# A second batch's queries turned by DMA instead of on TensorE, in a fused attention and feed-forward kernel

## The chip, the core and the metric

The kernel runs on one core of a Trainium2 chip. A core has TensorE (PE, with its weight loads shown apart as PEld), VectorE (DVE), ScalarE (ACT), GpSimd (POOL) and SyncE (SP), each with an instruction queue of its own, and 16 DMA engines that move data between memories. Matmuls read SBUF and write PSUM. The metric is the device time of one execution in microseconds (us); lower is better. The profile is of one execution: its span runs from the first to the last instruction.

## What is computed

Linear attention without a softmax on q, k, v of shape (batch 8, heads 8, sequence 576, head width 64), a normalization per head, and then a feed-forward network on the 4608 tokens with 512 features:

```
kv  = einsum('bhsd,bhse->bhde', k, v)            # 64 x 64 per batch and head
o   = einsum('bhsd,bhde->bhse', q, kv)
x   = o / sqrt(mean(o*o, -1) + 1e-6) * g_norm    # heads side by side: 4608 x 512
a, b = x @ w1, x @ w2                            # 4608 x 1024 each
out = (a * b) @ w3 @ w_out                       # 4608 x 512
```

The weights come as 64-bit floats and are converted to fp32 on the chip, in integer steps. w3 and w_out are multiplied once into one matrix (w3o).

## The kernel before

A batch has 576 tokens: 512 form a group of their own, and the 64 left of each batch are joined, two batches at a time, to a ninth group. The groups run in the order 0 to 6, 8, 7. Ahead of group 0 a start-up stage converts weights, folds w3 and w_out, and does batch 0's attention.

**A group's stages.** `gates(T, p, ...)` (blocks p = 0 to 3) computes a quarter of the hidden features by a scheme of seven products in place of eight (`winograd`), whose matmuls are L620 in the profile. Inside a block the products follow one another as: first product, copied by ScalarE as p1; second, copied as p5; third, added on top of the first in PSUM, copied as u2; fourth; fifth, copied as u3; sixth; seventh. The copies are `keep` (L633) and are remembered in `copies["u2"]` and so on. A PSUM bank that was copied is added to by a later product, so that the third product waits for p1's copy, the fourth for p5's, the fifth for u2's and the seventh for u3's. u2 and u3 share one SBUF buffer: u3's copy waits until VectorE has used u2. VectorE adds the parts (c, L758) and multiplies a and b (L755, L759). After the four blocks of group 0 comes its projection (`project`), later groups have `project_twice`.

**The next batch's attention inside a group.** `winograd` calls `between()` twice, and each call runs the next of eight places of `steps(T + 1)`. `steps` fills lists: `fs[i]` holds what is begun at place i, and `ends[i]` what is ended there, ahead of it. In group 0 the first block runs no places, so that the second block holds places 0 and 1, the third 2 and 3, the fourth 4 and 5, and the projection 6 and 7. For batch 1 the places hold: kv = k^T v of a pair of head pairs (`begin_kv`, L334, copied out of PSUM at L345); the queries turned, so that the head width lies along partitions (`begin_q` with `q_t`, L353, copied at L355; `q_t_left`, L370 and L371, for the 64 left of batches 0 and 1 together); the product of queries and kv with the normalization (`finish`, `product`, L417; `product_left`, L436); the result turned for the gates (`turn`, L451, or `x_by_dma`).

**The other way to turn.** From batch 2 on the queries are turned by DMA with `turn_by_dma` (L275). A generator in three steps: GpSimd copies the low and the high 16-bit halves of the fp32 words apart into two planes (L292, L294); SP issues a DMA transpose of 16-bit elements (L296); GpSimd copies the halves together again (L306). `q_two_by_dma` drives two of these and loads the next queries (`load_ahead`) in the third step.

**Weights.** `begin_next()` does ScalarE's part of a conversion (L159, L160), `end_next()` VectorE's part (L162 to L172), in group 0 with a scaling on ScalarE (L135), and loads the next raw weights. Four conversions are left for group 0: two after block 0, two after block 1 (L1312 to L1318). `sum_w(3)`, which needs the last two, is run after block 2 and serves block 3.

**Order.** TensorE, GpSimd and SP run in the order of the program. VectorE and ScalarE are ordered by a planner at compile time, which takes what it expects to be ready and prefers what the program lists first; `tc.issue_after(ins)` puts the instructions of the block behind `ins` on the engine of `ins`. From group 1 on, VectorE too follows the order of the program in each group's last block and projection. For odd batches (b = 1, 3, 5) `steps` hands VectorE's copy to the next batch's `begin_kv`, so that the kv of batches 2, 4 and 6, heads 0 to 3, are copied by VectorE; others are copied by ScalarE.

Of the kernel before, what the change touches and what calls it, by code (L numbers as in the profile page):

```python
# [4 lines left out]

# [8 lines left out]
FP32 = mybir.dt.float32  # L14
# [9 lines left out]
def kernel(  # L24
# [32 lines left out]
    nc = tc.nc  # L57
    PSUM = bass.MemoryType.PSUM
    P = 128
# [4 lines left out]
    NP = H // 2  # L64
# [19 lines left out]
    def bank(pool, tag):  # L84
        return pool.tile([P, 512], FP32, name=tag, tag=tag)


    loaded, copies = {}, {}
# [161 lines left out]
    def all_of(steps):  # L250
        for _ in steps:
            pass
# [19 lines left out]
        for _ in range(n):  # L272
            nc.tensor.matmul(t[:, 0:P], lhsT=ident, rhs=ident, start=True, stop=True)

    def turn_by_dma(srcs, apart, turned, dsts):  # L275

        def words(t):  # L280
            return t.bitcast(U16).rearrange("p ... (n w) -> p ... n w", w=2)

        def planes(t, i, n):
            t = t.bitcast(U16).rearrange("p (w n) -> p w n", w=2)
            size = 4 * P // n
            return t[:, :, i * size:(i + 1) * size]

        for i, src in enumerate(srcs):
            to = planes(apart, i, len(srcs))
            if len(src.shape) == 3:  # L290
                src, to = words(src), to.rearrange("p w (a n) -> p w a n", a=src.shape[1])
                nc.gpsimd.tensor_copy(to, src.rearrange("p a n w -> p w a n"))  # L292
            else:
                nc.gpsimd.tensor_copy(to, words(src).rearrange("p n w -> p w n"))  # L294
        yield
        nc.sync.dma_start_transpose(  # L296
            out=turned.bitcast(U16).rearrange("p (a t) -> p a t", t=P), in_=apart.bitcast(U16)
        )
        yield
        for i, dst in enumerate(dsts):  # L300
            src = planes(turned, i, len(dsts))
            if len(dst.shape) == 3:
                src = src.rearrange("p w (a n) -> p a n w", a=dst.shape[1])
            else:
                src = src.rearrange("p w n -> p n w")
            nc.gpsimd.tensor_copy(words(dst), src)  # L306

    def together(turns):

# [6 lines left out]
    def attention(b):  # L316
        kv_b = kv_sb[b % 3]
        qT = {}

        def start():  # L320
            xT[b] = work.tile([P, 2, 2, NP // 2, N], FP32, name="xT")

        def kv(rs, copy=nc.scalar.copy):


            n = len(rs)
            kv_ps = bank(ps_at, "at")[:, 0:n * D].rearrange("p (r d) -> p r d", d=D)
            for r in rs:
                k_sb, v_sb = loaded["k", b, r], loaded["v", b, r]
                kl, vl = kv_left  # L330
                for j in range(J + 1):
                    cols = slice(j * D, (j + 1) * D)
                    for e in range(2):
                        nc.tensor.matmul(  # L334
                            kv_ps[e * D:(e + 1) * D, r - rs[0], :],
                            lhsT=k_sb[:, e, cols] if j < J else kl[:, 2 * r + e, :],
                            rhs=v_sb[:, e, cols] if j < J else vl[:, 2 * r + e, :],
                            start=(j == 0),
                            stop=(j == J),
                        )  # L340
            for e in range(2):
                for i in range(2):
                    dst = kv_b[i * D:(i + 1) * D, e, rs[0]:rs[0] + n, :]
                    src = kv_ps[e * D:(e + 1) * D]
                    copy(dst, src)  # L345

        def q_t(r):

# [8 lines left out]
        def q_by_dma(r):  # L357

            qT[r] = work.tile([P, 2, 2, P], FP32, name="qT")
            q_sb = loaded["q", b, r].rearrange("p e n -> p (e n)")  # L360
            to = qT[r].rearrange("p e i t -> p (e i t)")
            return turn_by_dma([q_sb], to, q_sb, [to])

        st = {}

        def q_t_left():
            st["qT"] = work.tile([P, NP, P], FP32, name="qT_left", bufs=1)
            qt_ps = bank(ps_at, "at").rearrange("p (r t) -> p r t", r=NP)
            for r in range(NP):
                nc.tensor.transpose(qt_ps[:, r, :], q_left[b // 2][:, 2 * r:2 * r + 2, :], ident)  # L370
            nc.scalar.copy(st["qT"], qt_ps)  # L371

        def q_left_by_dma():
            st["qT"] = work.tile([P, NP, P], FP32, name="qT_left", bufs=1)
            src = q_left[b // 2].rearrange("p h d -> p (h d)")
            to = st["qT"].rearrange("p r t -> p (r t)")
            return turn_by_dma([src], to, src, [to])

        def norm(o_ps, dsts):

# [102 lines left out]
                if r + 1 == NP and "k" in names:  # L483
                    load_kv_left(b + 1)

        def begin_kv(*rs, **how):
            kv(rs, **how)
            for r in rs:
                load_ahead("kv", r)

# [14 lines left out]
        def finish(h):  # L505
            all_of(product(h))

        return SimpleNamespace(**{f.__name__: f for f in (
            start, begin_kv, begin_q, product, finish, turn, q_t_left, product_left,
            q_two_by_dma, q_left_by_dma, x_by_dma, x_left_by_dma,  # L510
        )})

# [2 lines left out]
    def batch(b):  # L515
        if b not in batches:
            batches[b] = attention(b)
        return batches[b]

    def steps(b):  # L520

        a = batch(b)
        a.start()
        more = b + 1 < B
        fs, ends = ([[] for _ in range(8)] for _ in range(2))

        def turn(i, f, *args, next_group=False):  # L530

            t = []

            def begin():
                t.append(f(*args))
                next(t[0])
                next(t[0])

            fs[i].append((begin,))
            (to_end if next_group else ends[i + 1]).append((lambda: all_of(t[0]),))  # L540

        if to_end:

            ends[0] += [(lambda: nc.gpsimd.tensor_copy(tick, late["p5"][:, 0, 0:1]),), *to_end]
        to_end.clear()
        odd = b % 2
        if b == 1:
            fs[0] += [(a.begin_kv, 0, 1), (a.begin_q, 0, 1)]
        fs[1] += [(a.begin_kv, 2, 3), (a.finish, 0)]
        if b == 1:  # L550
            fs[2] += [(a.q_t_left,), (a.begin_q, 2, 3)]
            fs[3] += [(a.turn, 0), (a.turn, 1)]
        else:
            turn(1, a.q_two_by_dma, 2, 3)
            turn(2, a.x_by_dma, 0)
            if odd:
                turn(1, a.q_left_by_dma)
        second = 5 if b == 1 else 4
        if more:
            how = dict(copy=nc.vector.tensor_copy) if odd else {}  # L560
            fs[second].append((partial(batch(b + 1).begin_kv, **how), 0, 1))
        fs[second].append((a.finish, 1))
        if odd:
            fs[second].append((a.product_left,))
        if b == 1:
            turn(6, a.x_by_dma, 1)
            turn(7, a.x_left_by_dma, next_group=True)
        else:
            turn(5, a.x_by_dma, 1)
            if odd:  # L570
                turn(5, a.x_left_by_dma, next_group=more)
        if more:
            turn(7 if b == 1 else 5, batch(b + 1).q_two_by_dma, 0, 1, next_group=True)
            fs[7 if odd else 0].append((load_q_left, b + 1))
        return iter([lambda s=e + f: [f(*args) for f, *args in s] for e, f in zip(ends, fs)])

    to_end = []


    w3T = {}  # L580
# [683 lines left out]
    for n, T in enumerate(groups):  # L1264
        pieces = steps(T + 1) if n + 2 < NG else iter([])

        def between():
            next(pieces, lambda: None)()
            if T == 1:
                for _ in range(2):  # L1270
                    if next(preparing, 0) == 0 and len(loaded_b) < 3:
                        load_b()
            if T == B - 2 and p == 2 and not replaced:
                replaced.append(True)
                replace_a21()
# [11 lines left out]
        for p in range(NF):  # L1287
            if T in TWICE and p + 1 < NF:
                continue
            if T and p + 1 == NF:  # L1290
# [16 lines left out]
                gates(T, p, between, lambda name: all_of(f() for f in following[name]))  # L1307
                continue
            gates(T, p, between if T or p else lambda: None)
            if T == 0:  # L1310
                if p + 1 < NF:
                    run(sum_w(p + 1))  # L1312
                for n in range(2):
                    if len(converted) < len(todo):
                        ahead = [copies["xT"] if p == 0 else copies["u3"][0], copies["u2"][p]][n]
                        with tc.issue_after(ahead.ins):
                            begin_next()
                        end_next()  # L1318
                if p + 1 == NF:
                    allocate_projection()  # L1320
                    run(*(f(i) for i in range(NF) for f in (sum_ab, combine_w3o)))
            else:
                ops = [step() for step in sum_ab(p)]
                with tc.issue_after(ops[-1].ins):
                    for _ in range({(3, 1): 2, (3, 2): 2, (4, 1): 2, (4, 2): 1}.get((T, p), 0)):
                        next(preparing_w)
# [43 lines left out]
```

## Time and profile before

| | |
|---|---|
| three timed runs, us | 762.75, 763.65, 763.81 (median 763.65) |
| span of the profiled execution, us | 762.3 |
| group 0's gates and projection | about 85 to 168 us |
| TensorE's granted clock | full throughout |
| L353, transposes of queries | 32 in all (16 in the start-up stage), 278 ns mean |
| L355, L371: copies of these from PSUM, ScalarE | 8 at 594 ns, 1 at 597 ns |
| L345, kv copies | 52 on ScalarE, 260 ns mean |
| DMA transposes (L296) | 57, SP's queue |

In the profile's lines, L12 is line 12 of the kernel; a group reads: line, engine, operation, output<-inputs, shapes, count, and busy time or mean. A timeline's line begins with start and length in us, and its bracket tells how long the engine was idle before and what ended that. "PE at" is TensorE writing a bank of the pool `at` (attention), "PE mm" one of the pool `mm`. Busy durations of TensorE's instructions overlap, so that eight transposes of 0.27 us each can pass in less than 1 us of the chain.

### The profile page before, as it was taken

The page shows a single profiled execution, that of the slowest core. Times are in us where ns is not written, and L with a number is a line of the kernel's source. Part 1 is how long each engine was busy: PE and PEld are TensorE (multiplying, and loading weights), DVE is VectorE, ACT ScalarE, POOL GpSimd, SP SyncE. Part 2 cuts the span into 40 slices and gives each one's busy share as a digit, 9 for nine tenths or more (in the row PEclk, how much of TensorE's full clock was granted, in tenths as well). Part 3 has the DMA queues.
Part 4 walks back from the last instruction along what each step waited for, and adds up shares of the span by engine and source line. Part 5 has one row for each costly group of instructions (what it writes and reads, how often), then busy time and mean ns, then how long its engine had stood idle before and what let it go on. Part 6 is the DMA issues. An engine that isn't in the chain of part 4 may idle for free.

```text
span 762.3 us, 15002 instructions
## 1 busy us (share of the span) xinstructions
PE 753.6 (99%) x5943; PEld 661.1 (87%) x5943; DVE 593.9 (78%) x1183; ACT 251.7 (33%) x471; POOL 165.2 (22%) x190
## 2 busy tenths in 40 slices
PE   7999999999999999999999999999999999999998
PEld 5455788888899889988998899889988999999997
DVE  7977999548879468948984998467867777996897
ACT  6776764213321322233222222332233223222321
POOL 0000000123520442043204420432053115006100
PEclk9999999999999999999999999999999999999999
DMA  9996642328998935685668467835652471456244
GB/s 312 342 329 207 205 124 57 84 70 262 319 275 293 240 98 155 238 210 152 192 229 219 147 185 232 209 104 157 229 135 54 139 223 49 145 201 194 85 148 142
DMA packets 137049, 140.83 MB, mean 185 GB/s; under 512 B 77076, under 2 KB 124308, under 8 KB 136980
## 3 DMA queue, kind: packets, MB, share of 16 engines
q1 hardware_dynamic: 134528, 125.46, 55.5%
q10 hardware_dynamic: 2452, 14.42, 5.5%
q8 instruction: 47, 0.77, 0.4%
q14 instruction: 22, 0.18, 0.1%
HBM read 105.78 MB, written 19.14 MB: 164 GB/s over the span
## 4 chain that ended last, share of the span: by engine, by line
PE 96%; DMA 2%; DVE 1%; ACT 0%; issue 0%; SPq 0%; ACTq 0%
PE mm L620 54%; PE mm L1049 22%; PE mm L599 7%; PE mm L849 5%; PE at L334 3%; PE at L417 2%; DMA raw<-in_moe_w_out_dram 1%; PE at L849 1%; DMA w3o_sb<-w3o_l 1%; PE at L586 1%; PE at L353 1%; PE at L1100 0%; DVE kv_sb L345 0%; DMA raw<-in_moe_w_dram 0%; PE at L451 0%; PE at L436 0%
## 5 line engine op out<-in xcount | busy, mean ns | idle before, releaser
L620 PE MATMUL mm<-xT,w_sb 128*128 128x256 f32 x720 | 165.2, 379 | 0.0
L620 PEld LDWEIGHTS mm<-xT,w_sb 128*128 128x128 f32 x720 | 136.3, 190 | 18.7 <-issue 0.5
L620 PE MATMUL mm<-xc,ws 128*128 128x256 f32 x512 | 115.7, 379 | 0.0
L620 PEld LDWEIGHTS mm<-xc,ws 128*128 128x128 f32 x512 | 97.2, 190 | 13.3
L758 DVE TENSOR_TENSOR c<-mm,u 128x512 f32<-128x512 f32 x32 | 22.0, 688 | 63.2 <-PE mm L620 63.2
L292 POOL COPY xT<-xn 128x1024 uint16<-128x1024 uint16 x26 | 31.6, 1244 | 177.9 <-DVE xn L395 177.9
L633 ACT COPY u<-mm 128x512 f32<-128x512 f32 x58 | 34.1, 587 | 99.2 <-PE mm L620 90.6
L633 ACT COPY p<-mm 128x512 f32<-128x512 f32 x66 | 38.7, 586 | 77.9 <-PE mm L620 75.0
L599 PE MATMUL mm<-chunks,ab 128*128 128x512 f32 x128 | 60.3, 603 | 2.0 <-ACT ab L591 1.3
L620 PE MATMUL mm<-xc,w_sb 128*128 128x256 f32 x256 | 61.4, 383 | 0.0
L620 PE MATMUL mm<-xT,ws 128*128 128x256 f32 x240 | 57.3, 382 | 0.0
L759 DVE TENSOR_TENSOR ab<-c 128x256 f32<-128x256 f32 x96 | 54.3, 566 | 2.5
L620 PEld LDWEIGHTS mm<-xc,w_sb 128*128 128x128 f32 x256 | 47.8, 190 | 6.9 <-ACT u L633 0.3
L620 PEld LDWEIGHTS mm<-xT,ws 128*128 128x128 f32 x240 | 44.9, 190 | 6.2
L1049 PE MATMUL mm<-w3o_sb,ab 128*128 128x128 f32 x368 | 48.7, 275 | 0.0
L1049 PE MATMUL mm<-w3o_sb,raw 128*128 128x128 f32 x372 | 48.1, 275 | 0.3 <-DMA w3o_sb<-w3o_l 0.3
L1049 PEld LDWEIGHTS mm<-w3o_sb,ab 128*128 128x128 f32 x368 | 45.4, 192 | 0.5
L1049 PEld LDWEIGHTS mm<-w3o_sb,raw 128*128 128x128 f32 x372 | 44.7, 192 | 0.4 <-issue 0.4
L754 ACT COPY c<-mm 128x256 f32<-128x256 f32 x32 | 11.9, 373 | 95.6 <-PE mm L620 95.6
L306 POOL COPY xT<-xn 128x1024 uint16<-128x1024 uint16 x26 | 31.9, 1254 | 52.5 <-DMA xn<-xT 52.5
L599 PEld LDWEIGHTS mm<-chunks,ab 128*128 128x128 f32 x128 | 21.8, 190 | 24.6 <-issue 16.5
L386 DVE TENSOR_REDUCE inv<-sq 128x8 f32<-128x512 f32 (+1 forms) x40 | 23.4, 626 | 24.2 <-ACT sq L385 24.2
(298 smaller groups left out, 1365.4 us busy)
## 6 DMA issues: line engine op xcount, KB each, us to landing
w3o_sb<-w3o_l SPq DMA_DIRECT2D x18, 896.0 KB, 5.5
raw<-in_moe_w_dram SPq DMA_DIRECT2D x31, 512.0 KB, 7.4
raw<-w3o_l SPq DMA_DIRECT2D x15, 896.0 KB, 4.6
w3o_sb<-w3o_l ACTq DMA_DIRECT2D x14, 896.0 KB, 4.5
k_sb<-in_k_dram SPq DMA_DIRECT2D x32, 256.0 KB, 3.6
v_sb<-in_v_dram SPq DMA_DIRECT2D x32, 256.0 KB, 4.8
q_sb<-in_q_dram SPq DMA_DIRECT2D x32, 256.0 KB, 4.2
out_dram<-raw SPq DMA_DIRECT2D x14, 512.0 KB, 3.6
```

The lines of the kernel that those rows point to most:

```text
L292: nc.gpsimd.tensor_copy(to, src.rearrange("p a n w -> p w a n"))
L306: nc.gpsimd.tensor_copy(words(dst), src)
L334: nc.tensor.matmul(kv_ps[e * D:(e + 1) * D, r - rs[0], :], lhsT=k_sb[:, e, cols] if j < J else kl[:, 2 * r + e, :], rhs=v_sb[:, e, cols] i ...
L386: nc.vector.tensor_reduce(out=inv[:, i], in_=sq.rearrange("p (h d) -> p h d", d=D), axis=AX.X, op=ALU.add)
L417: nc.tensor.matmul(o_ps[l][tokens, n * D:(n + 1) * D], lhsT=qT[r][rows, e, i, tokens], rhs=kv_b[rows, e, r, :], start=True, stop=True,)
L599: nc.tensor.matmul(sums_ps[half][m], lhsT=w3T[half, c][:, m, :], rhs=chunks[:, c, 1, :], start=(c == 0), stop=(c == KF - 1),)
L620: nc.tensor.matmul(ps[:, u, :], lhsT=lhsT(a_name, u, c), rhs=rhs(b_name, c),  start=(u == 0 and c == 0 and to is None), stop=(c == chunks ...
L633: copies.setdefault(name, []).append(nc.scalar.copy(t, ps))
L758: nc.vector.tensor_add(c, one, two)
L759: nc.vector.tensor_mul(dst, c[:, 0, :], c[:, 1, :])
L849: nc.tensor.matmul(ps[place // 4][:, place % 4, :], lhsT=x, rhs=y, start=new and place // 4 not in seen, stop=True, skip_group_check=True,)
L1049: nc.tensor.matmul(to[:, i, :], lhsT=x[:, c, :], rhs=y[:, c, :], start=new and place // 4 not in seen, stop=(c == 1), skip_group_check=True,)
```

## The change

Batch 1's queries and the leftover queries of batches 0 and 1 are no longer turned on TensorE but by DMA, as for later batches, with the copies apart and together on ScalarE in place of GpSimd:

- The first two head pairs are begun after block 0 (copies apart behind the last xT copy of batch 0, then the DMA transposes) and ended at place 1, behind kv's copies. The load of the next queries moves to there.
- The other two are begun at place 2, behind the third block's u2, and ended at place 4, behind the copies of `turn`; the leftover ones are begun at place 3, behind u3, and ended at place 4, behind p5.
- `q_t_left` is gone, and for batch 1 `begin_q` is not called (batch 0 still uses it).

The last of the weights' conversions begins after block 1 as before; its `end_next()` moves from there into the first `between()` of block 2, behind u2. And `begin_kv` has no choice of engine any more: ScalarE copies all kv.

```diff
-    def turn_by_dma(srcs, apart, turned, dsts):
+    def turn_by_dma(srcs, apart, turned, dsts, copy=nc.gpsimd.tensor_copy):
...
-                nc.gpsimd.tensor_copy(to, words(src).rearrange("p n w -> p w n"))
+                copy(to, words(src).rearrange("p n w -> p w n"))
...
     def attention(b):
+        q_copy = nc.scalar.copy if b == 1 else nc.gpsimd.tensor_copy
...
-        def kv(rs, copy=nc.scalar.copy):
+        def kv(rs):
...
-                    copy(dst, src)
+                    copies["kv"] = nc.scalar.copy(dst, src)
...
-            return turn_by_dma([q_sb], to, q_sb, [to])
+            return turn_by_dma([q_sb], to, q_sb, [to], q_copy)
...
         if b == 1:
-            fs[0] += [(a.begin_kv, 0, 1), (a.begin_q, 0, 1)]
+            q_first = a.q_two_by_dma(0, 1)
+            early.append(q_first)
+            fs[0].append((a.begin_kv, 0, 1))
+
+            def end_first():
+                with tc.issue_after(copies["kv"].ins):
+                    next(q_first)
+                all_of(q_first)
+
+            ends[1].append((end_first,))
         fs[1] += [(a.begin_kv, 2, 3), (a.finish, 0)]
         if b == 1:
-            fs[2] += [(a.q_t_left,), (a.begin_q, 2, 3)]
+            q_last = []
+
+            def begin(n, name):
+                q_last.append(a.q_left_by_dma() if n else a.q_two_by_dma(2, 3))
+                with tc.issue_after(copies[name][-1].ins):
+                    next(q_last[n])
+                next(q_last[n])
+
+            def end(n, name):
+                with tc.issue_after(copies[name].ins if n == 0 else copies[name][-1].ins):
+                    next(q_last[n], None)
+                all_of(q_last[n])
+
+            fs[2].append((begin, 0, "u2"))
+            fs[3].append((begin, 1, "u3"))
+            ends[4] += [(end, 0, "xT"), (end, 1, "p5")]
             fs[3] += [(a.turn, 0), (a.turn, 1)]
...
         if more:
-            how = dict(copy=nc.vector.tensor_copy) if odd else {}
-            fs[second].append((partial(batch(b + 1).begin_kv, **how), 0, 1))
+            fs[second].append((batch(b + 1).begin_kv, 0, 1))
...
         def between():
+            if len(converted) < len(begun):
+                with tc.issue_after(copies["u2"][-1].ins):
+                    end_next()
             next(pieces, lambda: None)()
...
             gates(T, p, between if T or p else lambda: None)
+            if T == 0 and p == 0:
+                for t in early:
+                    with tc.issue_after(copies["xT"].ins):
+                        next(t)
+                    next(t)
...
                         with tc.issue_after(ahead.ins):
                             begin_next()
-                        end_next()
+                        if len(begun) < len(todo):
+                            end_next()
```

More of the change, by code (lines that the diff above doesn't have):

```diff
@@ L1 @@
 from contextlib import ExitStack
-from functools import partial
 from itertools import islice
@@ L291, in turn_by_dma @@
                 src, to = words(src), to.rearrange("p w (a n) -> p w a n", a=src.shape[1])
-                nc.gpsimd.tensor_copy(to, src.rearrange("p a n w -> p w a n"))
+                copy(to, src.rearrange("p a n w -> p w a n"))
             else:
-                nc.gpsimd.tensor_copy(to, words(src).rearrange("p n w -> p w n"))
+                copy(to, words(src).rearrange("p n w -> p w n"))
         yield
@@ L305, in turn_by_dma @@
                 src = src.rearrange("p w n -> p n w")
-            nc.gpsimd.tensor_copy(words(dst), src)
+            copy(words(dst), src)
     def together(turns):
@@ L361, in q_by_dma @@
             to = qT[r].rearrange("p e i t -> p (e i t)")
-            return turn_by_dma([q_sb], to, q_sb, [to])
+            return turn_by_dma([q_sb], to, q_sb, [to], q_copy)
         st = {}
[L366 to L371, printed above, removed]
         def q_left_by_dma():
@@ L376, in q_left_by_dma @@
             to = st["qT"].rearrange("p r t -> p (r t)")
-            return turn_by_dma([src], to, src, [to])
+            return turn_by_dma([src], to, src, [to], q_copy)
         def norm(o_ps, dsts):
@@ L484, in load_ahead, with begin_kv @@
                     load_kv_left(b + 1)
-        def begin_kv(*rs, **how):
-            kv(rs, **how)
+        def begin_kv(*rs):
+            kv(rs)
             for r in rs:
@@ L508, in attention @@
         return SimpleNamespace(**{f.__name__: f for f in (
-            start, begin_kv, begin_q, product, finish, turn, q_t_left, product_left,
+            start, begin_kv, begin_q, product, finish, turn, product_left,
             q_two_by_dma, q_left_by_dma, x_by_dma, x_left_by_dma,
@@ L575, in steps @@
         return iter([lambda s=e + f: [f(*args) for f, *args in s] for e, f in zip(ends, fs)])
-    to_end = []
+    to_end, early = [], []
     w3T = {}
```

## The prediction

> **What bounds the kernel now.** I read the page first: busy time, the slices, the chain.
>
> ```profile
> PE 753.6 (99%) x5943; PEld 661.1 (87%) x5943; DVE 593.9 (78%) x1183; ACT 251.7 (33%) x471; POOL 165.2 (22%) x190
> ...
> PE   7999999999999999999999999999999999999998
> ...
> PE 96%; DMA 2%; DVE 1%; ACT 0%; issue 0%; SPq 0%; ACTq 0%
> ```
>
> TensorE is busy for all but 8.7 us of the 762.3 us span, and 96% of the chain that ends last is TensorE. So what leaves TensorE's list shortens the end, unless another engine then makes it wait. The change sits in group 0, about 82 to 142 us, so next I took the chain there, in order of time (start, length, what):
>
> ```profile
> 102.00 1.31 PE at L334 x40
> 103.32 1.02 PE at L353 x8
> 104.34 5.18 PE mm L620 x24
> 109.53 1.32 PE at L334 x40
> 110.84 1.09 PE at L417 x64
> 111.93 7.11 PE mm L620 x32
> 119.04 0.44 PE at L370 x4
> 119.48 0.87 PE at L353 x8
> 120.35 5.18 PE mm L620 x24
> ```
>
> The transposes of batch 1's queries (L353) and leftover queries (L370) are links of the chain, back to back with the gates (L620). Third, what TensorE waits for, over the whole span:
>
> ```profile
> PE at L436 <- DVE kv_sb L345: 1.0, 3, 0.4
> ```
>
> Three times product_left (L436) waits for a PSUM bank until VectorE has copied the next batch's kv out of it. Fourth, busy time by stage (length, then PE, PEld, DVE, ACT, POOL), to see who has room:
>
> ```profile
> 84.70:102.00 17.30, 17.30 (x83) 14.95 (x83) 17.30 (x27) 10.42 (x15) 0.00 (x0) 1.00 0.20 64
> ...
> 112.00:120.40 8.40, 8.40 (x45) 7.42 (x46) 8.40 (x17) 5.14 (x10) 0.00 (x0) 1.00 0.56 145
> 120.40:126.40 6.00, 6.00 (x33) 5.35 (x32) 6.00 (x18) 1.77 (x4) 0.00 (x0) 1.00 0.28 87
> 126.40:138.50 12.10, 12.10 (x59) 10.37 (x59) 8.49 (x21) 3.40 (x7) 0.00 (x0) 1.00 0.01 1
> ```
>
> VectorE is full until about 132, ScalarE is not, GpSimd does nothing, and DMA is nearly quiet after 120. Last, ScalarE's timeline, for the size of its gaps:
>
> ```profile
> 119.13 0.59 ACT L633 COPY u<-mm 128x512 f32<-128x512 f32 x1 [1.20 <-PE mm L620]
> 119.61 0.60 ACT L371 COPY qT_left<-at 128x512 f32<-128x512 f32 x1
> 120.09 1.09 ACT L355 COPY qT<-at 128x512 f32<-128x512 f32 x2
> 124.99 0.59 ACT L633 COPY u<-mm 128x512 f32<-128x512 f32 x1 [3.80 <-DVE c L758]
> 126.01 1.07 ACT L453 COPY xT<-at 128x512 f32<-128x512 f32 x2 [0.43 <-PE at L451]
> ```
>
> **What the Trainium skill says.** "TensorE: Matmul & The Clock Gate", Part 4: PE-mode transpose, gives about 275 ns for a 128x128 transpose inside a kernel. The trace agrees (L353: 278 ns mean), but they overlap: 8 take 0.87 to 1.02 us of the chain, and only that can be saved. "DMA: Bandwidth & Descriptors", DMA Transpose (X-bar), allows 2-byte types only, on the SP and ScalarE queues. That is why fp32 queries must be copied apart into two planes before the transpose and together after it; here the transposes are SP's L296 and the copies are 128x1024 uint16. "ScalarE: Activation LUTs", What ACT_TABLE_LOAD costs, prices an ACTIVATE with immediate scale at 186 ns + 0.833 ns per element and lets neighbours overlap by some 93 ns. For 1024 elements that is an estimate of 1.04 us; the trace's nearest rows are longer (L135 and L160, 128x1024 fp32: 1.15 to 1.18 us, starting 1.06 apart in a row), so I use 1.15 us, and 2.2 us for a pair.
>
> **Part 1: 20 transposes leave TensorE.** 8 of L353 in the first place, 4 of L370 and 8 of L353 in the second: 1.02 + 0.44 + 0.87 = 2.33 us. None of it lies beside other TensorE work. From 104.3 on everything on TensorE is 1.02 us earlier, from 120.3 on 2.33 us.
>
> **Part 2: ScalarE.** It loses five copies of 0.59 us (L355, L371: 2.95 us) and gets ten uint16 copies, 11.5 us at 1.15: +8.5 us in a stretch (82 to 133) where its gaps add up to about 20 us. No run here shows a uint16 copy on ScalarE. Bounds: 1.04 us (the skill's price) and 2.3 us (half rate, if two-byte strided elements cost double). I take 1.15 because GpSimd's rows for these very copies lie at 1.2 us, near the count of elements.
> Where each goes, on the clock of after:
> - First pair behind xT's last copy (82.0): in the queue with two w3o copies, one L159 and one L160 before the first gate copy (p at 86.50). p is needed when the third product starts, about 88.05, so it has 0.95 us to spare. The pair displaces L159 and L160, which were ready early for VectorE. I take 0; at worst one copy's length, 1.1.
> - Its end behind kv's copies (105.84): to 108.0, against 106.9 before. product(0) starts at 110.84 - 1.02 = 109.8: 1.8 us to spare. Queued behind: L135 and L159 (2.1 us), then u3, at worst done at 110.8; it is needed at 110.9. I take 0.
> - Second pair behind the third block's u2 (119.13 - 2.33 + 0.59 = 117.4) and the scaling L135 moved there (1.06): 118.5 to 120.7. The gap of 3.8 us was here; u3, queued behind, is due at 121.6. Cost 0.
> - Leftover queries behind u3 (122.2 to 123.3), before xT's copies at 123.7: 0.
> - Ends: the pair behind xT's copies (124.9 to 127.1), before p of the fourth block at 127.6; the leftover behind p5 (129.9 to 131.0), before u2 at 131.1: 0, but here ScalarE can stand still for a DMA (rival 2).
>
> **Part 3: DMA and SP.** Five DMA transposes of 1.25 to 1.45 us issue on SP. A pair was delivered 4.3 us after its first issue in a quiet stretch:
>
> ```profile
> 147.60 2.70 SPq L296 DMA_TRANSPOSE xn<-xT  x2
> 151.93 1.14 POOL L306 COPY xT<-xn 128x1024 uint16<-128x1024 uint16 x1 [4.36 <-DMA xn<-xT]
> ```
>
> (Two views: SP's timeline and GpSimd's.) First pair: issued about 86, landed by about 91, used at 105.8. Second: issued 120.7, landed 125.0; its end copies start at 124.9 at the earliest: 0.1 us of waiting. Leftover: landed by 127, used at 129.9. Behind the first transposes on SP stands the last weights' load (issued at 85.10 before; 7.4 us to land), now at about 88, landed by 96, first read at 102.6: hidden. q(1,2) and q(1,3) load at 108.2 instead of 105.97, land in 4.2 us, and are used at 118.5. Batch 2's queries load at 127 instead of 119.94, and are used at 155. GpSimd's queue gets nothing of this.
>
> **Part 4: last conversion.** The four VectorE instructions of the last conversion keep their number (L162, L166, L169, L172: about 3.6 us); they are listed behind the third block's u2, and only ScalarE's scaling is held to u2. sum_w(3) then can start at 118.5 and takes 4 x 0.6; its first sum is needed when the fourth block's second product starts, 129.8 - 2.3 = 127.5. Hidden, 0; it frees ScalarE of 1.06 us just before p of the third block, which in the trace came with only 0.15 us to spare.
>
> **Part 5: kv copies of batches 2, 4, 6 move from VectorE to ScalarE.** At 277.5 and 429.4 VectorE copies in 1.20 us and TensorE starts 0.14 later, 0.28 after product(1) is done. ScalarE's four copies take 1.08 after 0.05 (at 201.46): 0.10 less, twice. At 140, VectorE began 0.26 late behind gate work; ScalarE is idle: 0.28. Sum 0.48 us. If ScalarE were late here, 0 or -0.5.
>
> **Sum.** 2.33 + 0.48 = 2.81 us off the span of 762.3, so 759.5. The three timed runs have a median of 763.65, 1.35 above this span; I carry the difference over: 763.65 - 2.8 = 760.9. Later stages follow TensorE: x for group 1 is ready at 158.5 for gates that start near 168, and the only later DMA wait is 0.3 us.
>
> **Rivals.**
> 1. VectorE hands the gain back. It is full to 132. In the trace the third block's c (L758) started at 124.22 behind 4 us of sums for the projection (L662, L672, L673), and u3's copy waited for it ("3.80 <-DVE c L758") until 125.6. Should the new order leave c there, the last product of the third block, due at 126.41 - 2.33 = 124.08, starts at 125.7: 1.6 us of the 2.81 are lost: 762.4. For: the 100% above. Against: those sums are not due until after 139, VectorE has 3.6 us idle between 132.7 and 138, and c is listed ahead of them.
> 2. ScalarE becomes the bound (the slower side). Place: the end pair behind xT's copies, with p of the fourth block queued behind. p must be copied by 131.43 - 2.33 = 129.1, so the pair must start by 126.3; I expect 125.0. At 2.3 us a copy: second pair 118.5 to 122.9, landed 127.2, ended 131.6, p 132.2: TensorE waits 3.1 us. The same price costs 0.6 at product(0) and 1.1 at the first block's p and 0.1 at the last u2: 4.9 - 2.8 = 2.1 us slower, 765.7. It outweighs the gain from about 1.8 us a copy. For: nothing shows two-byte copies on ScalarE. Against: price and GpSimd's rows.
> 3. The change doesn't take effect where TensorE waits: the transposes were hidden. Time 763.6. Against: they are links of the chain with no idle TensorE about them.
>
> **How the numbers follow.** Sum as worked out, 0.66 (own range 760.3 to 762.0: wait left over up to 1.1, and up to 0.6 more should the kv waits vanish); rival 1, 0.19; rival 2, 0.11; rival 3, 0.04. A measurement of this kernel can tell 0.2%, 1.5 us: 762.1 and 765.2 are the borders. Faster: 0.66 and a third of rival 1, 0.72. Slower: rival 2 without a little that falls inside the border, 0.09. Same: 0.19. Range 760.1 to 763.9: above it lies rival 2, below it little.
>
> **What would show it.** No L353 or L370 in group 0, and 2.3 us less between 102 and 142 with TensorE without idle time; uint16 rows on ScalarE near 1.15 us; no wait of ScalarE for a DMA above 0.5 us; L436's wait near 0.5 in total. Wrong if TensorE shows waits for ScalarE or for c between 86 and 135, or if those rows are near 2 us.

## The result, and the profile after

The changed kernel takes 761.09 us (median of six runs, 760.47 to 762.54) where the kernel before takes 763.73 (six runs, 762.75 to 764.73). The ratio is 0.9967, with a 95% interval of 0.9953 to 0.9981, so it is faster by 2.6 us, between 1.5 and 3.6. 760.9 was predicted. The profiled execution spans 758.8 us, 3.5 less than that of before; the sum of the prediction had 759.5.

The page of the changed kernel, busy time and chain:

```profile
PE 751.2 (99%) x5923; PEld 658.9 (87%) x5923; DVE 586.7 (77%) x1171; ACT 261.6 (34%) x488; POOL 165.6 (22%) x190
...
PE 97%; ACT 1%; DMA 1%; DVE 0%; SPq 0%; issue 0%; ACTq 0%
```

TensorE has 20 instructions fewer and is 2.4 us less busy, ScalarE is 9.9 us busier, and GpSimd is as before. The chain of group 0, over the places that the prediction showed of before (lines have moved: the gates are L636 now, `product` is L410, `turn` is L444):

```profile
101.89 1.31 PE at L334 x40
103.21 5.38 PE mm L636 x24
108.59 1.37 PE at L334 x40
109.95 1.09 PE at L410 x64
111.05 12.28 PE mm L636 x56
123.33 0.87 PE at L444 x8
```

Both links of transposes are gone and nothing stands in their place. Note the 5.38 us for 24 gate matmuls: they took 5.18 while transposes stood ahead of them. TensorE's waits over the whole span are now three, all in the start-up stage:

```profile
PE mm L272 <- POOL ident masks.py:199: 2.0, 1, 2.0
PE mm L615 <- DVE chunks L171: 1.6, 1, 1.6
PE mm L615 <- ACT ab L607: 0.4, 1, 0.4
```

The waits of product_left for kv_sb are gone, and so is the one for a DMA of w3o_sb. ScalarE's timeline, at the place that the prediction showed (L293 copies apart, L305 together, L134 is the last scaling):

```profile
118.24 0.59 ACT L649 COPY u<-mm 128x512 f32<-128x512 f32 x1 [1.20 <-PE mm L636]
118.72 1.15 ACT L134 ACTIVATE w_sb<-w_sb,g_col 128x1024 f32<-128x1024 f32 x1
119.78 1.98 ACT L293 COPY qT<-q_sb 128x1024 uint16<-128x1024 uint16 x2
123.34 0.59 ACT L649 COPY u<-mm 128x512 f32<-128x512 f32 x1 [1.59 <-PE mm L636]
123.83 1.05 ACT L293 COPY qT_left<-ql_sb 128x1024 uint16<-128x1024 uint16 x1
124.77 1.07 ACT L446 COPY xT<-at 128x512 f32<-128x512 f32 x2
125.73 2.24 ACT L305 COPY qT<-q_sb 128x1024 uint16<-128x1024 uint16 x2
```

The gap of 3.8 us is filled with the scaling and the pair, and 1.6 us of it are left. These are not spare. The bracket names TensorE, but TensorE's timeline has the fifth product done near 121.5, and u3's copy (123.34) begins 0.10 us after the end of VectorE's c, as it did before (c from 124.22 for 0.68, u3 at 124.99):

```profile
122.55 0.69 DVE L774 TENSOR_TENSOR c<-mm,u 128x512 f32<-128x512 f32 x1
```

The pair together starts at once behind xT's copies: its DMA had landed, and ScalarE doesn't stand still for it.

To tell stages apart in every kernel, I took the starts of TensorE's rows from the timelines. Columns, in us: A from the first gates to kv of pairs 0 and 1; B from there to kv of pairs 2 and 3 (holds the first place of transposes); C on to the next batch's kv (holds the second place and block 3); D on to product_left; E from the second kv in group 1 to the first in group 2 (holds group 1's projection, with its DMA waits). A wait that the list shows costs more in these stretches than its idle time: in e3, 1.61 us of idle time lengthen C by 1.87. The eight matmuls ahead of the wait end 0.16 us after the next would have started in an unbroken row, and the eight behind it take 1.99 us in place of 1.89.

| kernel | A | B | C | D | E | span | ratio to before (95%) |
|---|---|---|---|---|---|---|---|
| before | 17.36 | 7.52 | 28.97 | 2.92 | 54.47 | 762.3 | |
| changed | 17.38 | 6.69 | 27.76 | 2.56 | 53.89 | 758.8 | 0.9967 (0.9953 to 0.9981) |
| changed again (e0) | 17.37 | 6.69 | 27.76 | 2.56 | 54.61 | 758.8 | 0.9968 (0.9956 to 0.9980) |
| e1, kv copies only | 17.35 | 7.52 | 28.99 | 2.56 | 53.97 | 760.8 | 0.9992 (0.9983 to 1.0000) |
| e2, kv on VectorE again | 17.37 | 6.69 | 27.76 | 2.92 | 54.12 | 760.0 | 0.9980 (0.9967 to 0.9992) |
| e3, conversion back | 17.37 | 6.69 | 29.63 | 2.56 | 54.21 | 760.4 | 0.9992 (0.9982 to 1.0003) |
| e4, no ties | 17.77 | 6.69 | 28.86 | 2.56 | 55.42 | 762.8 | 1.0014 (0.9998 to 1.0030) |
| e5, copies twice | 17.90 | 6.69 | 29.50 | 2.56 | 53.99 | 760.5 | 1.0008 (0.9994 to 1.0022) |
| e6, GpSimd copies | 17.69 | 6.70 | 31.21 | 2.61 | 53.88 | 762.1 | 1.0018 (1.0010 to 1.0026) |
| e7, x by DMA too | 17.37 | 6.69 | 31.13 | 2.56 | 54.98 | 763.8 | 0.9999 (0.9986 to 1.0011) |
| e8, conversion only | 17.36 | 7.52 | 28.96 | 2.92 | 54.16 | 762.1 | 0.9999 (0.9991 to 1.0007) |
| e9, sums behind c | 17.37 | 6.69 | 28.59 | 2.56 | 55.44 | 761.2 | 0.9981 (0.9973 to 0.9988) |
| e10, x and sums | 17.36 | 6.69 | 27.72 | 3.12 | 54.22 | 759.3 | 0.9975 (0.9965 to 0.9985) |
| e11, x and order | 17.37 | 6.69 | 27.02 | 2.56 | 54.30 | 759.0 | 0.9951 (0.9934 to 0.9969) |

So the 3.5 us of the two first profiles are: B 0.83, C 1.21, D 0.36, E 0.58, 0.17 for product_left in group 2, 0.17 for that in group 4, 0.07 in what else follows, and 0.13 that the start-up was quicker (A is 0.02 longer).

### The profile page after: what moved, and what is told of

It reads as the page before. It is cut to its first block, busy times and chain, and to the rows that moved or that the text cites. A ratio compares the mean times of both kernels' runs of the same rounds, so it can differ in the third digit from the quotient of the medians.

```text
span 758.8 us, 14978 instructions
## 1 busy us (share of the span) xinstructions
PE 751.2 (99%) x5923; PEld 658.9 (87%) x5923; DVE 586.7 (77%) x1171; ACT 261.6 (34%) x488; POOL 165.6 (22%) x190
## 4 chain that ended last, share of the span: by engine, by line
PE 97%; ACT 1%; DMA 1%; DVE 0%; SPq 0%; issue 0%; ACTq 0%
PE mm L636 55%; PE mm L1065 23%; PE mm L615 7%; PE mm L865 5%; PE at L334 3%; PE at L410 2%; PE at L865 1%; PE at L602 1%; DMA raw<-in_moe_w_out_dram 1%; PE at L1116 0%; PE at L444 0%; ACT ab L158 0%; ACT chunks L159 0%; PE at L353 0%; PE at L429 0%; SPq L196 0%
## 5 line engine op out<-in xcount | busy, mean ns | idle before, releaser
L636 PE MATMUL mm<-xT,w_sb 128*128 128x256 f32 x720 | 165.2, 379 | 0.0
L636 PEld LDWEIGHTS mm<-xT,w_sb 128*128 128x128 f32 x720 | 136.3, 190 | 18.6 <-issue 0.5
L636 PE MATMUL mm<-xc,ws 128*128 128x256 f32 x512 | 115.8, 379 | 0.0
L636 PEld LDWEIGHTS mm<-xc,ws 128*128 128x128 f32 x512 | 97.2, 190 | 13.4 <-ACT p L649 0.2
L774 DVE TENSOR_TENSOR c<-mm,u 128x512 f32<-128x512 f32 x32 | 22.0, 688 | 58.8 <-PE mm L636 58.8
L636 PE MATMUL mm<-xc,w_sb 128*128 128x256 f32 x256 | 61.5, 383 | 0.0
L636 PE MATMUL mm<-xT,ws 128*128 128x256 f32 x240 | 57.4, 382 | 0.0
L775 DVE TENSOR_TENSOR ab<-c 128x256 f32<-128x256 f32 x96 | 53.6, 558 | 2.5
L636 PEld LDWEIGHTS mm<-xc,w_sb 128*128 128x128 f32 x256 | 47.8, 190 | 7.0 <-ACT u L649 0.3
L636 PEld LDWEIGHTS mm<-xT,ws 128*128 128x128 f32 x240 | 45.0, 190 | 6.3
L305 POOL COPY xT<-xn 128x1024 uint16<-128x1024 uint16 x26 | 32.2, 1266 | 53.7 <-DMA xn<-xT 53.7
```

Of the source, the lines that this page charges most:

```text
L636: nc.tensor.matmul(ps[:, u, :], lhsT=lhsT(a_name, u, c), rhs=rhs(b_name, c),  start=(u == 0 and c == 0 and to is None), stop=(c == chunks ...
L774: nc.vector.tensor_add(c, one, two)
L775: nc.vector.tensor_mul(dst, c[:, 0, :], c[:, 1, :])
```

## The experiments

**The changed kernel again.** No edit.

> The changed kernel once more, beside the kernels that undo parts of it. Its first profile fell 3.5 us below the profile of before: 2.1 us for the transposes (0.83 in the first place, 1.32 in the second), 0.7 for the three waits of product_left, 0.6 for a DMA wait of w3o_sb in group 1's projection that was gone, 0.1 in the start-up. Theory: the transposes and the waits are the change, 2.8 us; the DMA wait comes and goes by itself. Then this profile shows the same group 0 to 0.1 us, and the DMA wait may be back. Rival: the DMA wait went because of the change (its loads follow SP's and ScalarE's queues), and it is gone again in this profile and in every profile with the change. Time 760.5 to 762.5.

A to D are the same to 0.01 us. The DMA wait is back, with no edit:

```profile
PE mm L1065 <- DMA w3o_sb<-w3o_l: 0.5, 1, 0.5
```

The span is the same because the start-up was 0.7 us quicker this time. Over all kernels E runs from 53.88 to 55.44 with no relation to the edits (e9, with VectorE's order changed in group 0 alone, has the longest). So the 0.58 us of E in the first pair of profiles are not the change's; it was right to leave this out of the sum.

**Only the kv copies** (e1), and **all but the kv copies** (e2).

```diff
# e1, from the kernel before
-            how = dict(copy=nc.vector.tensor_copy) if odd else {}
+            how = {}
# e2, from the changed kernel: kv takes copy again, and
-            fs[second].append((batch(b + 1).begin_kv, 0, 1))
+            how = dict(copy=nc.vector.tensor_copy) if odd else {}
+            fs[second].append((partial(batch(b + 1).begin_kv, **how), 0, 1))
```

> The kernel before, and only the kv copies of batches 2, 4 and 6 moved to ScalarE. Theory: product_left's three waits (0.36 + 0.17 + 0.17 us by the two first profiles) go, 0.7 us: 763.0 beside 763.7. Rival: these waits were incidental to the order of group 0, and the move alone is worth under 0.2 us; then they stay in the list of TensorE's waits.

> The changed kernel, with these kv copies on VectorE again. Theory: the three waits come back at 1.0 us in all (0.7 more than the changed kernel has), 761.8 beside 761.1; the transposes' gain is independent of them. Rival: all of the change's gain hangs on these copies, 763.5.

TensorE's waits in e2:

```profile
PE at L430 <- DVE kv_sb L346: 1.1, 3, 0.4
```

The three waits come back with the copies on VectorE, and none is listed in e1. D is 2.92 with VectorE and 2.56 with ScalarE, whether the transposes are there or not, and B and C don't care. By the ratios the copies are worth 0.6 us (e1, interval 0.0 to 1.3) and the rest 1.5 us (e2, 0.6 to 2.5). Within these intervals the parts add up; the stretches say it more sharply.

**The last conversion back where it was** (e3), and **only the conversion moved** (e8).

```diff
# e3, from the changed kernel
-                        if len(begun) < len(todo):
-                            end_next()
+                        end_next()
# e8: these lines, and those of between(), put into the kernel before
```

> The changed kernel, with the last conversion ended after block 1 as before. Prediction's step: that move costs and gains nothing by itself on TensorE but gives ScalarE 1.06 us ahead of p of the third block. If that room was needed, TensorE waits up to 1.0 us for p or u2 in the third block (762.1); if the planner finds a place for the scaling anyway, group 0 is the same to 0.1 us and the time is 761.1. I expect the second.

> The kernel before, and only the last conversion ended in block 2 as the change has it. Putting it back cost the changed kernel 1.6 us in one wait for p of the third block, because the scaling stood ahead of p on ScalarE and had to wait for VectorE. Theory: in the kernel before TensorE came 1.0 us later to that place and p was in time by 0.15 us, so that the move alone is worth nothing: within 0.3 us of before (763.4), no wait in group 0. Rival: the move has a gain of its own of about 1.5 us, 762.

I expected no difference from e3, and it loses 1.87 us in C. TensorE's timeline, and ScalarE's at that place:

```profile
117.54 1.99 PE L636 MATMUL mm<-xc,ws 128*128 128x256 f32 x8 [1.61 <-ACT p L649]
```

```profile
115.86 1.15 ACT L134 ACTIVATE w_sb<-w_sb,g_col 128x1024 f32<-128x1024 f32 x1 [0.82 <-DVE w_sb L171]
116.92 1.05 ACT L649 COPY p<-mm 128x512 f32<-128x512 f32 x2
```

The scaling stands in ScalarE's queue ahead of p, waits 0.82 us for VectorE's last step of the conversion, and takes 1.06; the third product waits for p (the copy p1 of the first product). In the changed kernel p is copied at 115.49 and the scaling comes behind u2. Alone, the move is worth nothing (e8: C 28.96 beside 28.97, ratio 0.9999). So it is the condition under which most of the transposes' gain is had, not a gain of its own.

Two things differ at that place between e3 and the kernel before, and no run separates them. TensorE comes some 0.8 us earlier (A and B together are 24.06 us, not 24.88). And VectorE's order is another one: before, and in e8, the conversion's last step ran ahead of the reduction for product(0) (112.83 and 114.64 before), and in the kernel before the scaling was done before the root that follows the reduction; in e3 the planner put that step behind the reduction (113.43, then 114.62), so that the scaling came between the root and p.

**No ties for the query copies** (e4): the four `with tc.issue_after(...)` around them are left out.

> The changed kernel without the ties: the query copies on ScalarE go where the planner puts them. Theory: ScalarE runs in order, so a copy together that is listed ahead of its DMA's landing holds the gate copies behind it. First pair ahead of p of block 0: landed about 87, p done at 89.0 where it is needed at 88.05, TensorE waits about 1 us; second pair between p5 and u2 of block 2: landed about 118.4, u2 done at 121.2 where the fifth product needs it at 119.6, 1.6 us. Together 2.6 us: 763.7. Rival: the gaps are wide enough wherever the copies stand, 761.1, with no wait of ScalarE for a DMA.

The interval of the ratio holds what was expected (no gain left), but the places are only partly the expected ones. ScalarE waits for the landing of transposes, which it never does in the changed kernel:

```profile
ACT qT L305 <- DMA q_sb<-qT: 1.4, 2, 0.8
```

That costs 0.4 us in A and 1.1 in C. One more us is lost where I had not looked: the planner put the first copies apart ahead of the squares of batch 0's product, and `turn` waited 0.94 us for xn in the start-up stage (E's 55.4 is the DMA wait, and not the edit's).

**Every query copy twice** (e5).

```diff
-        q_copy = nc.scalar.copy if b == 1 else nc.gpsimd.tensor_copy
+        def copy_twice(dst, src):
+            nc.scalar.copy(dst, src)
+            nc.scalar.copy(dst, src)
+
+        q_copy = copy_twice if b == 1 else nc.gpsimd.tensor_copy
```

> The changed kernel with each of the ten query copies on ScalarE done twice, which stands for a copy of 2.2 us. By the prediction's second rival TensorE then waits 3.1 us at p of the fourth block, 0.6 at product(0), 1.1 at the first block's p and 0.1 at the last u2: 4.9 us over the changed kernel, 766.0. If the gaps take more than was thought, less: each place that is off by more than 0.5 us tells that its room was misjudged.

A and C are longer by 0.53 and 1.74: 2.3 us in place of 4.9. With that the change's gain is spent (0.9994 to 1.0022). The big term, 3.1 us at p of the fourth block, was wrong for this kernel: the planner does not queue a copy and its repetition behind one another but puts p between them (copy at 128.22, p at 129.28, its repetition at 129.76). A copy done twice is not one copy of twice the length, so the price from which rival 2 decides stays open; what is shown is that some 10 us more on ScalarE in this stretch use up the gain.

**GpSimd in place of ScalarE** (e6): `q_copy` is GpSimd's copy for every batch.

> The changed kernel with the query copies on GpSimd, at the same places of the program. If ScalarE is not what the gain needs, TensorE loses the same 20 transposes and GpSimd, idle until 143 us, has the time: 761.1, and ScalarE is 11 us less busy. Rival: GpSimd's copies beside a full VectorE make VectorE's instructions longer, or come late since GpSimd follows the program, and TensorE waits for product(0) or c: 762 to 764.

The rival came true: slower than before. VectorE's timeline in e6, and the same instructions in the changed kernel (L775 multiplies two SBUF operands, L171 adds two):

```profile
113.30 1.25 DVE L775 TENSOR_TENSOR ab<-c 128x256 f32<-128x256 f32 x1
114.48 2.05 DVE L171 CUSTOM_DVE_ANT_0 w_sb<-w_sb,ab 128x2048 uint16<-128x2048 uint16 x1
```

```profile
112.70 0.42 DVE L775 TENSOR_TENSOR ab<-c 128x256 f32<-128x256 f32 x1
115.16 1.22 DVE L171 CUSTOM_DVE_ANT_0 w_sb<-w_sb,ab 128x2048 uint16<-128x2048 uint16 x1
```

While GpSimd copies (111.30 to 115.4), each is 0.83 us longer. "SBUF — State Buffer" of the Trainium skill, section SBUF: two separate sides, says that a VectorE operation with two SBUF inputs and a GpSimd operation that reads SBUF lock each other out of a shared port pair; the trace agrees in kind (c, L774, with one operand in PSUM, kept its 0.68 us at 111.86), with 0.83 us a time as the amount. It is not only such instructions: beside the first pair's copies together, the scaling L136, which has one operand and a column, took 1.65 us in place of 0.75, and GpSimd's two copies took 7.26 us.

VectorE is full there, so its reduction for product(0) and then ScalarE's root come 2.5 us later than in the changed kernel (117.75, not 115.28), p behind the root, and TensorE waits 1.60 us for p. Not all of this is the longer instructions: the planner also put the conversion's last step (L171) ahead of the reduction here, behind which it stands in the changed kernel, and in e9 that order alone makes p 1.0 us late. No run has GpSimd's copies with the other order. TensorE waits 0.44 us more for u3, and 0.77 us for v of the second kv. That load was issued at 104.97, earlier than in the changed kernel (105.36), but took 4.6 us to land and not 3.7; here the loads of q followed it at once (105.54, not 107.13). Whether they slowed it stays open: in the kernel before they followed as closely, and v took 3.8.

**x's first half by DMA as well** (e7), **the sums held back** (e9), **both** (e10).

```diff
# e7, from the changed kernel
-            fs[3] += [(a.turn, 0), (a.turn, 1)]
+            turn(2, a.x_by_dma, 0)
# and the end of the second pair tied behind the leftover's copy apart
# e9, from the changed kernel (the c's addition is kept as copies["c12"])
-                    run(*(f(i) for i in range(NF) for f in (sum_ab, combine_w3o)))
+                    with tc.issue_after(copies["c12"][2].ins):
+                        run(*(f(i) for i in range(NF) for f in (sum_ab, combine_w3o)))
```

> The changed kernel, and batch 1's first half of x turned by DMA as well (copies on GpSimd) in place of eight transposes of TensorE (L444) and two copies of ScalarE. Theory: what is in TensorE's list between products counts in full, 8 x 0.109 = 0.87 us less: 760.2, and ScalarE has 1.1 us more room. x is needed by VectorE at about 132.5 and is ready by about 127. Rival: GpSimd's four copies slow the full VectorE, or x comes late, and the 0.87 us are lost in waits.

> The changed kernel, with VectorE's sums for the projection (L688, L689, L678 on raw and w3o_sb) held behind the third block's c of c12. In the changed kernel c starts at 122.55 though it is ready at about 120, and u3's copy ends 0.1 us before the seventh product needs it. Theory: this is margin, not time: c starts about 2 us earlier, the time is that of the changed kernel within 0.3 us (761.2). Rival: the sums, begun later, are late for the projection and TensorE waits near 143: 1 us or more slower.

> e7 (x's first half turned by DMA with GpSimd's copies) with the sums held behind c as in e9. In e7 TensorE waited 2.4 us for u3, because c stood behind these sums, which GpSimd's copies made longer. Theory: with c ahead of them that wait goes and eight transposes leave TensorE for good: 0.87 us under the changed kernel, 760.4 and the fastest of all. Rival: VectorE, lengthened by GpSimd, is short in the whole stretch, and the wait comes back at c of a later block or at the projection: 761.5 to 763.

e7 lost where 0.87 was to be gained. TensorE's timeline, and the stretch 125 to 129 of the view by windows (after the four engines' and GpSimd's busy time: granted clock, DMA share, GB/s):

```profile
125.75 3.40 PE L641 MATMUL mm<-xc,w_sb 128*128 128x256 f32 x8 [2.38 <-ACT u L654]
```

```profile
125.00:129.00 4.00, 3.25 (x9) 2.61 (x10) 4.00 (x9) 3.66 (x4) 1.16 (x1) 0.65 0.85 180
```

u3's copy waited for c, c stood on VectorE behind the sums for the projection, and two of those were lengthened by GpSimd. This is rival 1 of the prediction, in a kernel where TensorE comes 0.87 us earlier still. And the wait cost twice: behind 2.38 us of idle time the mean granted clock from 125 to 129 was 0.65 (0.50 from 127 to 129), and eight matmuls took 3.40 us in place of 1.89. Behind 1.61 us (e3) the clock stayed at 1.00. These are two cases; no run varies the idle time alone.

With the sums behind c (e9) c starts at 121.47 in place of 122.55, but C is 0.83 us longer: I had not expected that. The planner then put the conversion's last step (113.83) ahead of the reduction of product(0) (114.97), and with it ScalarE's root and p came 1.0 us late; v of the second kv, landed at 109.33, cost 0.2 us more. In e10 the wait for u3 is gone as expected, but p's remains (0.67 us), and the fourth block's u3 comes late behind the sums, with the kv copies behind it (D 3.12). C and D together are 0.5 us longer than in the changed kernel (30.84 beside 30.32); by the ratios the two can't be told apart.

**x by DMA, with the order mended** (e11).

```diff
# from e10
+        with tc.issue_after(copies["hold"].ins) if "hold" in copies else ExitStack():
             nc.vector.tensor_tensor(out=dst_bits, in0=dst_bits, in1=low_bits, op=ALU.add)
...
-                with tc.issue_after(copies["c12"][2].ins):
-                    run(*(f(i) for i in range(NF) for f in (sum_ab, combine_w3o)))
+                for two in range(2):
+                    with tc.issue_after(copies["c12"][2 + two].ins):
+                        run(*(f(2 * two + i) for i in range(2) for f in (sum_ab, combine_w3o)))
# copies["hold"] is product(0)'s last reduction, set around the last end_next()
```

> e10 with its two waits aimed at: the last integer step of the last conversion (L172) is held on VectorE behind the reduction of product(0), so that ScalarE's root (L387) and p behind it are in time (e10 waited 0.67 us there), and the sums of the last two quarters are held behind the fourth block's c instead of the third's, so that its u3 and the kv copies behind it are in time (0.55 us). Theory: TensorE has no wait in group 0 and the stretch from kv(2, 3) to the next product_left is 29.6 us, beside 30.3 in the changed kernel and 30.8 in e10: 0.7 us under the changed kernel, ratio about 0.996. Rival: what is pushed back on VectorE comes late for the projection near 142 (sums) or for x, and 0.5 us or more is waited there: ratio 0.997 or above.

C is 27.02 and D 2.56, 29.58 in all, as expected, and TensorE has no wait in group 0. The ratio is 0.9951 (0.9934 to 0.9969), the lowest of all, though its interval and that of the changed kernel overlap; what separates them is C, 0.74 us shorter. 0.22 us of it are given back between product_left and group 1's first kv (36.68 us in place of 36.46). They lie in group 0's projection, where 32 matmuls (`mm<-raw`) took 7.29 us in place of 7.07: the weight loads among them waited 0.35 us for ScalarE's p, which stood behind a root that waited for VectorE. So the rival, that what is pushed back on VectorE comes late, is there in small.

## Why the prediction held

**Part 1, the transposes.** 2.33 us were predicted and 2.04 came (B 0.83, C 1.21). The first place was counted 0.19 too high: some 0.15 of its 1.02 us, against 0.87 for the same 8 transposes in the second place, was the cost of going from the narrow kv matmuls to wide ones, and the gates that follow kv now pay it (5.38 us beside 5.18; their first eight matmuls take 1.99 us, and took 1.89 behind the transposes). In C the kv at its start and the gates behind `turn` are longer by some 0.06 us each.

**Part 2, ScalarE.** 1.15 us a copy were taken. The groups of the changed kernel:

```profile
L305 ACT COPY qT<-q_sb 128x1024 uint16<-128x1024 uint16 x4 | 4.5, 1174 | 0.0
L293 ACT COPY qT<-q_sb 128x1024 uint16<-128x1024 uint16 x4 | 4.1, 1054 | 0.0
```

Mean durations are 1.17 us together and 1.05 apart, and ScalarE was idle ahead of none of them: all five places fitted. The second pair was placed 1.3 us too early: 119.13 lies ahead of the second place of transposes, where TensorE has gained 1.02 us and not yet 2.33. Its copies apart began at 119.78, not at 118.5. Two margins were thinner than stated: u3 of the third block, due at 121.6 by the prediction, was copied at 123.34 and done at 123.93 for a product that starts at 124.04; p of the first block ended at 87.24, 0.7 us ahead.

**Part 3, DMA.** The second pair was issued at 120.83 and had landed by 125.73 at the latest; the 0.1 us of waiting did not show. One thing was missed: TensorE, being earlier, also comes closer to the landing of v for kv(2, 3). Before, this v landed at 109.18, and its matmuls began at 110.09; now it lands at 109.02, and they begin at 109.15. In e9 and e6 it was late (109.33 and 109.58), and they began 0.13 to 0.14 behind it.

**Part 4, the conversion.** As a term of the sum, 0 was right: p was in time. But the sum took for granted what e3 prices at 1.87 us, and the reason given was not the right one. The remark was that the move frees ScalarE ahead of p of the third block, where 0.15 us were to spare. Before, though, ScalarE was not short of room there. The scaling was done, and ScalarE stood idle until VectorE's reduction for product(0):

```profile
114.08 1.15 ACT L135 ACTIVATE w_sb<-w_sb,g_col 128x1024 f32<-128x1024 f32 x1 [1.01 <-DVE w_sb L172]
115.94 0.31 ACT L390 ACTIVATE inv<-inv,eps_col 128x16 f32<-128x16 f32 x1 [0.70 <-DVE inv L386]
```

So the 0.15 us hung on when that reduction ran on a full VectorE. Had VectorE kept its order and its times, p would have come some 0.6 us late for a TensorE that is 0.8 us earlier (an estimate: 0.8 less 0.15). In the changed kernel the planner took the reduction (113.97) ahead of the conversion's last step (115.16). e9 has the scaling behind u2 as well but the old order, and waits for p; e11 ties the new order, and doesn't. Two things kept p in time, then: the reduction first, and the scaling behind u2. The prediction named the second without a price and didn't name the first, so that the planner chose it was luck.

**Part 5, the kv copies.** 0.48 predicted; 0.36, 0.17 and 0.17 measured in groups 0, 2 and 4, 0.70 in all. At the later two I had left 0.18 us of waiting; there was none listed.

Parts 1 and 5 give 2.74 us where the sum had 2.81. That it came so close is in part luck: part 1 was 0.29 too high and part 5 0.22 too low. **Rival 1** half happened. The prediction held against it that c is listed ahead of the sums, but c of the third block started at 122.55, still behind sums. It was only 1.67 us earlier than before, with TensorE 2.2 us earlier, mainly because three of the fourth block's four weight sums now stand behind it (L689 at 123.15, 124.09 and 125.29), and u3 was in time by 0.11 us. No step of the prediction had foreseen this margin, and e7 shows what one push more does. **Rival 2**'s price is refuted by the rows; its place was not the one that gives first (e3, e6 and e9 all wait at p of the third block). **Rival 3** is refuted by B and C, which are the same in every kernel that drops the transposes and has no wait there.

## What to carry to other kernels

When TensorE is busy for 99% of the span, an instruction taken from its list counts at its share of the chain, not at its duration (0.11 us for a transpose of 0.27), and only as long as each copy that a PSUM bank waits for still comes in time. So list these copies with their margins first, in the clock of the changed kernel; where a margin is 0.15 us, an edit that is worth nothing by itself can be the condition for the rest. For each such copy ask which engine it really waits for: here ScalarE made the copy, but VectorE's order decided when. And where an engine runs in order, tie added work behind a copy that is due, with the landing of its DMA in mind, and look at which instructions another engine's work will lengthen before giving it to an idle engine.

## What the runs showed of the hardware

In e6, GpSimd's copies of 128x1024 uint16 made VectorE's instructions with two SBUF operands 0.83 us longer each (0.42 to 1.25, 1.22 to 2.05), and a scaling with one operand and a column 0.90 us longer (0.75 to 1.65), while c with one operand in PSUM kept its 0.68. And TensorE's granted clock was 0.65 in the mean over the 4 us that hold the restart after 2.38 us without matmuls (e7), and 1.00 after 1.61 (e3).
